# The last 224 rows of a weight in two transfers over 25 and 7 partitions instead of four over 8

## Chip, cores, metric

The kernel runs on one core of a Trainium2 chip. The metric is the device time of one execution in microseconds. Before the change it is 664.14 us, the median of 3 runs (664.11 to 664.20).

## The reference, cut to what matters

One decoding step: a cached attention block and a gated MLP read the same normalised `x`, and their outputs are added to `x`. Four sequences, one token each, 32 heads, 4096 cached positions of 128 values, all in bf16.

```python
def _A_ref(x, k_cache, v_cache, wq, wo):          # k_cache, v_cache: (4, 32, 4096, 128)
    ...                                           # q = x @ wq; softmax(q k^T) v; @ wo
def _B_ref(x, w_in, w_sp, b_sp, w_out):           # w_in: (640, 1728), w_out: (864, 640)
    z = _gelu(jnp.einsum('bsd,df->bsf', x, w_in))
    ...
    return jnp.einsum('bsf,fd->bsd', z1 * g, w_out)
xn = _layernorm(x, axis=-1)
return x + _A_ref(xn, ...) + _B_ref(xn, ...)
```

The two caches are 268 of the 282 MB that are read. The change touches the last 224 of the 864 rows of `w_out`, 0.29 MB.

## The kernel before

All large loads go out on one queue, in program order, into five slots of SBUF. The first 640 rows of `w_out` go to 128 partitions, five rows to each. The other 224 are 32 times 7 rows; they go to the lowest 32 partitions of a buffer that is later used for something else. They come in four transfers: transfer `r` covers partitions `r`, `r+4`, ..., `r+28`.

```python
FA = 5
FR = (Fh - FA * P) // 32                     # 7
# ...
nc.sync.dma_start(out=wq, in_=A_wq.rearrange("(p c) n -> p c n", c=DC))
# ...
nc.sync.dma_start(out=w_in, in_=B_w_in.rearrange("(p c) f -> p c f", c=DC))
nf = FA * P
# ...
nc.sync.dma_start(out=w_out, in_=B_w_out[0:nf, :].rearrange("(p c) n -> p c n", p=P))
w_rest_t = ktpool.tile([P, NKT], F32, tag="kT", name="w_rest")
w_rest = w_rest_t[:32].bitcast(BF16)[:, 0:FR * NOUT].rearrange("p (c n) -> p c n", c=FR)
# ...
w_rest_d = B_w_out[nf:Fh, :].rearrange("(i r c) n -> r i c n", r=4, c=FR)
for r in range(4):
    nc.sync.dma_start(out=w_rest[r:32:4], in_=w_rest_d[r])
# ...
load_unit(seq[0])                            # the first unit of k_cache, 8.39 MB
# ... much later: the only readers of w_rest
for fc in range(FC):
    # ...
    for hf in range(NH):
        nc.tensor.matmul(proj[...], lhsT=uT[:n, fc, 0:nb],
                         rhs=(w_out[:, fc] if fc < FA else w_rest[:, fc - FA])[:, hf * NO2:(hf + 1) * NO2], ...)
```

The rest of the kernel is a loop over 16 units of k and 16 of v, and at the end the projection with `wo`.

Of the kernel before, what the change touches and what calls it, by code (L numbers as in the profile page):

```python
# [16 lines left out]
def kernel(  # L17
# [19 lines left out]
    nc = tc.nc  # L37
# [18 lines left out]
    Fh = F2 // 2  # L56
    FA = 5
    FR = (Fh - FA * P) // 32
# [56 lines left out]
    nf = FA * P  # L115
# [3 lines left out]
    w_rest = w_rest_t[:32].bitcast(BF16)[:, 0:FR * NOUT].rearrange("p (c n) -> p c n", c=FR)  # L119

    NB = 32 * FC
    z_at = n_in + FA * NOUT
    w_rest_d = B_w_out[nf:Fh, :].rearrange("(i r c) n -> r i c n", r=4, c=FR)
    for r in range(4):
        nc.sync.dma_start(out=w_rest[r:32:4], in_=w_rest_d[r])


    seq = [("k", u) for u in range(B)]
# [212 lines left out]
    for fc in range(FC):  # L341
        n = P if fc < FA else 32
        nb = B if fc > 1 else 32
        r0 = 64 * (fc % 2)
# [202 lines left out]
    for c in range(HG):  # L547

        p = part.get(c, 0)
# [41 lines left out]
```

## Time and profile before

| | before |
|---|---|
| time | 664.14 us |
| span of the profiled run | 662.5 us |
| read from memory | 282.25 MB, 426 GB/s over the span |
| busiest compute engine | DVE, 54% |
| last piece of `wo` landed | 658.98 us |

The prediction below shows the lines of the page that say what bounds the kernel.

Some numbers below come from the records of single DMA packets and of single semaphore counts (one for each engine that has finished its part of a transfer), which stand in the trace. Of such counts a large load has 16, each of the four small transfers 8, each of the two loads of `x_res` 4. The records don't name the engine; the strands, of which the prediction speaks, are my own stringing by time. "Loss" of a strand means: the time from the end of its last `w_out` packet to the end of its eighth packet of the first k load, less eight times 2.414 us. In the kernel before it is 1.37 us on the eight strands with small packets and 0.01 us on the other eight.

### The profile page before, as it was taken

What the parts mean: (1) busy time and instruction counts of PE and PEld (TensorE: products, weight loads), DVE (VectorE), ACT (ScalarE), POOL (GpSimd) and SP (SyncE); (2) the same over time, 40 slices, a digit from 0 to 9 for tenths busy, and PEclk for the clock granted to TensorE, in tenths of its full rate; (3) what the DMA queues carried; (4) which work ended last, traced back from release to release, by engine and by line L of the source; (5) the groups of instructions that cost most, each with busy time, mean ns of one, the idle gap of its engine ahead of it and who ended that gap; (6) DMA issues with size and microseconds to landing.
All of it is one profiled execution on the core that took longest, in us unless ns stands there. A gap on an engine that the chain in (4) does not pass through costs nothing.

```text
span 662.5 us, 5421 instructions
## 1 busy us (share of the span) xinstructions
PE 292.9 (44%) x2297; PEld 106.5 (16%) x2297; DVE 360.1 (54%) x275; ACT 78.4 (12%) x162; POOL 20.3 (3%) x64
## 2 busy tenths in 40 slices
PE   0636666256072556225336054533506254623245
PEld 0111122112021122111112022111202112211122
DVE  2249899556191759618256286745619185951112
ACT  0300000530100000530200000071010000053200
POOL 6210000000000000000000000000000000000000
PEclk9858768678577587677859596756958759667767
DMA  9999999999999999999999999999999999999996
GB/s 371 463 424 427 426 444 437 435 436 416 443 432 423 439 418 442 433 439 440 423 420 435 432 421 452 433 424 431 431 436 444 428 431 415 445 432 437 418 419 262
DMA packets 6901, 282.61 MB, mean 427 GB/s; under 512 B 808, under 2 KB 1084, under 8 KB 1468
## 3 DMA queue, kind: packets, MB, share of 16 engines
q1 hardware_dynamic: 6856, 282.25, 98.8%
q8 instruction: 18, 0.29, 0.2%
q14 instruction: 7, 0.06, 0.0%
q10 hardware_dynamic: 20, 0.01, 0.0%
HBM read 282.25 MB, written 0.01 MB: 426 GB/s over the span
## 4 chain that ended last, share of the span: by engine, by line
DMA 74%; DVE 11%; issue 11%; PE 2%; ACT 1%; SPq 0%; DVEq 0%; ACTq 0%
DMA kv<-in_A_k_cache_dram 64%; DVE kT L367 11%; DMA kv<-in_A_v_cache_dram 5%; DMA kv<-in_A_wo_dram 3%; DMA kv<-in_A_wq_dram 2%; PE O L449 2%; ACT xd L432 0%; ACT Zb L413 0%; ACT p L421 0%; DVE pT L425 0%; PE last_a L553 0%; DVE m L385 0%; PE S L378 0%; SPq L169 0%; PE misc L390 0%
## 5 line engine op out<-in xcount | busy, mean ns | idle before, releaser
L367 DVE STREAM_TRANSPOSE kT<-kv 128x2048 f32<-128x2048 f32 x128 | 282.8, 2276 | 124.7 <-DMA kv<-in_A_k_cache_dram 124.7
L378 PE MATMUL S<-kT,QZ 128*32 128x512 bf16 x1024 | 187.9, 500 | 230.6 <-DVE kT L367 230.6
L378 PEld LDWEIGHTS <-QZ 128*32 128x32 bf16 x1024 | 60.3, 111 | 353.4 <-issue 332.6
L449 PE MATMUL O<-kv,Zb 128*32 128x512 bf16 x1024 | 73.6, 451 | 58.2 <-DMA kv<-in_A_v_cache_dram 38.0
L458 DVE TENSOR_TENSOR om<-O,Mk 128x512 f32<-128x512 f32 x15 | 10.4, 692 | 109.0 <-PE O L449 109.0
L413 ACT ACTIVATE Zb<-xd,MkE 32x256 bf16<-32x256 bf16 x116 | 52.9, 498 | 110.4 <-PE O L449 109.0
L421 ACT ACTIVATE p<-S,negmax 128x512 bf16<-128x512 f32 x8 | 5.4, 683 | 400.6 <-DVE negmax L399 400.6
L449 PEld LDWEIGHTS <-Zb 128*32 128x32 bf16 x1024 | 32.9, 112 | 97.4 <-issue 55.8
L472 PE MATMUL misc<-R,SelR 128*32 128x128 f32 x32 | 6.4, 281 | 30.0 <-DVE R L459 28.4
L353 POOL COPY QZ<-qT 32x32 bf16<-32x32 bf16 x16 | 5.1, 318 | 390.6 <-PE S L378 389.9
L432 DVE COPY xd<-pT 32x256 bf16<-32x256 bf16 x44 | 16.0, 365 | 0.8
L459 DVE TENSOR_REDUCE R<-om 128x128 f32<-128x512 f32 x15 | 15.3, 1019 | 0.5
L432 ACT COPY xd<-pT 32x256 bf16<-32x256 bf16 x20 | 12.3, 614 | 5.6 <-DVE pT L425 5.2
L425 DVE STREAM_TRANSPOSE pT<-p 128x1024 bf16<-128x1024 bf16 x4 | 5.0, 1245 | 6.3 <-ACT p L421 6.3
L472 PEld LDWEIGHTS misc<-R,SelR 128*32 128x32 f32 x32 | 2.2, 107 | 37.8 <-DVE R L459 26.0
L385 DVE TENSOR_REDUCE m<-S 128x2 f32<-128x1024 f32 x4 | 4.9, 1225 | 5.5 <-PE S L378 5.5
L274 PE MATMUL q<-kv,xnT 128*32 128x512 bf16 x40 | 4.5, 630 | 6.9 <-DMA kv<-in_A_wq_dram 6.9
L461 DVE TENSOR_SCALAR R<-O,Mk 128x128 f32<-128x128 f32 x1 | 0.4, 351 | 12.5 <-PE O L449 12.5
L282 DVE CAST kv<-q 128x512 bf16<-128x512 f32 x1 | 0.7, 692 | 11.1 <-PE q L274 11.1
L390 PE MATMUL misc<-dg,ones_f 128*128 128x256 f32 x8 | 3.2, 488 | 7.6 <-DVE dg L387 7.6
L475 DVE SCALAR_TENSOR_TENSOR om<-misc,rinv,SelH 32x1024 bf16<-32x1024 f32 x4 | 5.1, 1271 | 2.0 <-PE misc L472 2.0
L437 PE MATMUL misc<-rowsum,SelPe 128*32 128x1 f32 x16 | 2.1, 202 | 9.0 <-ACT p L421 9.0
(102 smaller groups left out, 78.2 us busy)
## 6 DMA issues: line engine op xcount, KB each, us to landing
kv<-in_A_k_cache_dram SPq DMA_DIRECT2D x8, 4096.0 KB
kv<-in_A_v_cache_dram SPq DMA_DIRECT2D x1, 6144.0 KB
kv<-in_A_wq_dram SPq DMA_DIRECT2D x1, 5120.0 KB
kv<-in_A_wo_dram SPq DMA_DIRECT2D x3, 1280.0 KB
kv<-in_B_w_in_dram SPq DMA_DIRECT2D x1, 2160.0 KB, 19.9
kv<-in_A_v_cache_dram SPq DMA_DIRECT2D x1, 2048.0 KB
kv<-in_B_w_out_dram SPq DMA_DIRECT2D x1, 800.0 KB
kv<-in_A_wo_dram SPq DMA_DIRECT2D x1, 640.0 KB, 22.0
```

The lines of the kernel that those rows point to most:

```text
L353: nc.gpsimd.tensor_copy(out=QZ[r0:r0 + 32, :, :, :, 8 + 8 * hp], in_=qT[32 * g:32 * g + 32, NE * hp:NE * hp + NE].rearrange("p e a b -> p ...
L367: nc.vector.transpose(kT[:].rearrange("p (t r) -> p t r", r=32), kw)
L378: nc.tensor.matmul(S_ps[32 * q:32 * q + 32, e], lhsT=QZ[:, b, 2 * kh + w, e, w0:w0 + 32], rhs=kb[:, i, :, e, :, w], start=(b == 0 and k < ...
L413: nc.scalar.activation(out=dst, in_=src, func=ACT.Copy, scale=mk)
L421: nc.scalar.activation(out=p_bf[:, :, e, :], in_=S_ps[:, e], func=ACT.Exp, bias=negmax[:, e:e + 1], scale=scale, accum_out=rowsum[:, e:e + 1])
L425: nc.vector.transpose(pT[:].rearrange("p t h x -> p (t h x)"), p_bf[:].rearrange("p t e m -> p (t e m)"))
L432: op(out=xd[32 * hp:32 * hp + 32, :, q, :], in_=pT[32 * q:32 * q + 32, :, hp, :].rearrange("p t x -> p x t"))
L449: nc.tensor.matmul(O_ps[32 * q:32 * q + 32, :, :], lhsT=Zb[b % 2][:, w].rearrange("p h c -> p (h c)"), rhs=vv[:, w * 4 * Dh:(w + 1) * 4 * ...
L458: nc.vector.tensor_tensor(out=om4[:], in0=O_ps[:], in1=Mk4[:, :, None].to_broadcast((P, 4, Dh)), op=ALU.mult)
L459: nc.vector.tensor_reduce(out=R, in_=om4[:].rearrange("p c d -> p d c"), axis=AX.X, op=ALU.add)
L472: nc.tensor.matmul(oh[:], lhsT=SelR[:, b].rearrange("p h b -> p (h b)"), rhs=state["R"][:, b, :], start=(b == 0), stop=(b == B - 1))
L475: nc.vector.scalar_tensor_tensor(out=om[:], in0=oh[:, None, :].to_broadcast((G, HG, Dh)), scalar=state.pop(("rinv", g))[:, 0:1], in1=MkH[: ...
```

## The change

The intent: two transfers instead of four, over runs of partitions, with fewer issues. The four transfers over 8 partitions counted 8 landings each.

```diff
-    w_rest_d = B_w_out[nf:Fh, :].rearrange("(i r c) n -> r i c n", r=4, c=FR)
-    for r in range(4):
-        nc.sync.dma_start(out=w_rest[r:32:4], in_=w_rest_d[r])
+    w_rest_d = B_w_out[nf:Fh, :].rearrange("(p c) n -> p c n", c=FR)
+
+    for r0, r1 in ((0, 25), (25, 32)):
+        nc.sync.dma_start(out=w_rest[r0:r1], in_=w_rest_d[r0:r1])
```

The same rows land in the same partitions.

## The prediction

> **What bounds the kernel now.** I read the page from the top: slices, queues, chain; then the queue's own timeline, then the single packets and landings.
>
> From the page of the kernel before (the line of DMA is busy tenths per slice; the queue line is packets, MB, share of the time of 16 engines):
>
> ```profile
> DMA  9999999999999999999999999999999999999996
> q1 hardware_dynamic: 6856, 282.25, 98.8%
> DMA 74%; DVE 11%; issue 11%; PE 2%; ACT 1%; SPq 0%; DVEq 0%; ACTq 0%
> kv<-in_A_v_cache_dram SPq DMA_DIRECT2D x15, 29.5
> w_rest<-in_B_w_out_dram SPq DMA_DIRECT2D x4, 70.0 KB
> ```
>
> The 16 DMA engines work without a break on one queue, and DVE, the busiest engine, has 54%. A bulk load lands 29.5 us after its issue although its own 8.39 MB need 19.4 us (128 packets of 65,536 B, 8 on each engine, 2.418 us each): 10 us of earlier work are always ahead of it. So neither the issues nor DVE bound this kernel, but the bytes that one DMA engine has to move. A packet of 65,536 B takes 2.418 us all through the trace, which is 27.1 GB/s per engine[...].
>
> The chain of waits, its last stretch (start, length, what):
>
> ```profile
> 635.85 22.32 DMA kv<-in_A_wo_dram
> 658.17 0.04 issue
> 658.21 0.43 PE last_a L553 x2
> 658.64 0.01 PE misc L553 x2
> 658.65 0.82 PE last_a L553 x4
> 659.47 0.02 issue
> 659.49 0.48 DVE o_bf L560
> ```
>
> The end is the landing of the last piece of wo, two matmuls, an addition, and the store. Each transfer counts as landed when its slowest engine is through, and[...] the end belongs to **the engine that is furthest behind**, not to the mean.
>
> The start, from the timeline of the queue that issues (start, length with its waits):
>
> ```profile
> 0.73 0.39 SPq L110 DMA_DIRECT2D kv<-in_A_wq_dram  x1
> 1.18 0.42 SPq L113 DMA_DIRECT2D kv<-in_B_w_in_dram  x1
> 1.64 0.57 SPq L117 DMA_DIRECT2D kv<-in_B_w_out_dram  x1
> 2.25 14.30 SPq L125 DMA_DIRECT2D w_rest<-in_B_w_out_dram  x4
> 16.60 36.15 SPq L161 DMA_DIRECT2D kv<-in_A_k_cache_dram  x3
> ```
>
> The four small transfers of the change hold the issuing queue from 2.25 to 16.55 us. In the waits of that queue 11.5 us of this are a wait for wq: the semaphores of the transfers come round after eight, and the fourth small one needs the semaphore of wq.
>
> [...]each of the four transfers over 8 partitions counted 8 landings, x_res over 4 partitions 4, all others 16. [...]
>
> **The change part by part.** The 32 partitions hold 7 rows of 640 bf16, 8,960 B each; such a packet takes 338 ns, and the packet that counts the semaphore 9 ns.
> - Before, engines 0 to 7 each move 4 of them: 4 x (338 + 9) = 1.39 us that engines 8 to 15 don't have.
> - After, engines 0 to 4 move 5 + 1 = 6: 6 x 338 + 2 x 9 = 2.05 us, so **+0.66 us**. Engines 5 and 6 move 1: 0.35 us, so -1.04. Engine 7 moves none: -1.39. Bytes, packets of data and everything later are the same.
> - Two issues of some 0.63 us fall away, and the wait of 11.5 us with them, since the semaphore of wq is next needed by the second load of k_cache. The first k load can be issued near 3.6 instead of 16.6 us. It gains nothing: the engines reach that load at 21 to 23 us, the landing times of the small transfers show.
> - The consumer of w_rest is a group of 14 matmuls at 36.7 us, after a chain on ACT, DVE and POOL; w_rest lands by 23.8 us. Some 12 us of slack.
>
> So only the tail of the most loaded engine counts. The packets don't name their engine, but each starts 3 to 6 ns before the end of the one ahead, so they can be strung into 16 strands by time (my own working from the packet records). Eight strands carry w_rest, four of them x_res as well, so these are engines 0 to 3. All strands have the same bulk; they differ by a start spread over 1.1 us, by w_rest, and by instruction fetches of 16,384 B (about 1.0 us each) and 8,192 B (0.3 us) that fall on some. The last packets end at 658.57 us on the latest strand, then 658.26 (one of engines 0 to 3), 658.26 (one of 8 to 15), 658.22 and 658.11 (both of 4 to 7). The fastest end near 654. The latest owes its place to a third 16 KB fetch at 633.7 us; the fetches go round eight strands in a fixed order, and by it this is one of engines 8 to 15, though at 628 us two strands meet and could be exchanged.
>
> Engine cost alone: 658.26 + 0.66 = 658.92 against 658.57 now, **+0.35 us**; if the latest strand is one of 0 to 4, +0.66.
>
> **Rivals.**
> [...]
> - *A faster start.* The queue is free 13 us earlier. That would help only if an engine had run dry; no strand has a gap other than fetches. No change in time.
> - *A balance that helps.* If the latest strand were engine 5, 6 or 7, its end would fall back by 1.0 to 1.4, but 658.26 + 0.66 on the other strand remains. So hardly below 664.1; a gain needs fetches that fall otherwise.
> - *Knock-on through buffers.* A later first k load delays DVE, and with it the issue of the third load at 52.4 us. The fastest engine would need it near 60 us; 2 us are lost in that slack.
>
> **Range and chances.** I weigh engine cost alone (664.14 + 0.35 to 0.66, so 664.5 to 664.8) with a third[...], the rest for luck with fetches[...]. Middle: 665.2 us, range 664.0 to 667.0. A change of 2% is 13.3 us, more than six times the largest term: within 2% with 0.985, slower 0.01, faster 0.005.
>
> **What would show it.** The two transfers should count 5 and 7 landings, with 32 packets of 8,960 B. The wait of the issuing queue for wq at this line should be gone, the first k load issued near 3.6 us, and landed no earlier than 43 us. [...] The spread between first and last engine of a landing should grow by 0.3 to 2.5 us right after w_rest and stay; bulk packets should keep 2.418 us. The last piece of wo should land (658.98 us before) later by the change in time. I am wrong if the end moves though that spread doesn't, if a strand runs dry, or if k isn't 5 and 7.

One rival, +0.7 to +2.2 us (664.8 to 666.4 us): that the partitions which are written count too. It was the estimate from an assumption, and it had a little over half of the weight. The sum: engine cost alone with a third, that rival with a little over half, the rest for luck with fetches and for a worse case of the rival, in the middle 665.2 us, range 664.0 to 667.0. The "largest term" there is the rival's 2.2 us. `k` is the number of engines that a transfer runs on, to be read from its landings.

The numbers of engines are names, here and in the expectations: "engines 0 to 7" are the eight strands that carry small packets in the kernel before, "0 to 3" the four of them that carry `x_res` too, "8 to 15" the eight strands without small packets.

That the semaphores come round after eight can be seen in the trace of the kernel before: its first eight transfers, `x`, `wq`, the two single values, `w_in`, `w_out` and two of the small ones, have a semaphore each. The third small one has that of `x`, the fourth that of `wq`, on which `wq` counted from 14.86 to 15.92 us and the small one from 23.28 to 23.72.

## More of the kernel before

One more view is needed for what follows: the stretch from 21 to 26 us, in which the four small transfers and the start of the first k load pass. The columns are the stretch, its length, the busy time of PE, PEld, DVE, ACT and POOL (with instructions), the granted clock, the share of the DMA engines, and GB/s. The share goes over 1; packets seem to count where they start. So only equal stretches should be compared.

```profile
core 0: us, PE busy (x) PEld busy (x) DVE busy (x) ACT busy (x) POOL busy (x), PEclk, DMA share, GB/s
21.00:26.00 5.00, 4.93 (x25) 1.07 (x24) 1.40 (x2) 0.69 (x2) 1.57 (x5) 1.00 1.26 540
```

What to see: 540 is the figure of an undisturbed stretch, with which the others are compared.

## The result

The changed kernel takes 665.51 us, the median of 6 runs (665.14 to 665.75), against 664.12 us (664.06 to 664.31) of the kernel before. The ratio is 1.002 with a 95% interval of 1.0007 to 1.0033, so it is the same within 2%, and slower by 1.4 us. A ratio is the mean time of one kernel's fast runs over that of the other's of the same rounds, so it isn't quite the ratio of the medians.

From the page of the kernel after (tenths of DMA, the queue line, the chain):

```profile
DMA  9999999999999999999999999999999999999996
q1 hardware_dynamic: 6836, 282.25, 98.9%
DMA 74%; DVE 11%; issue 11%; PE 2%; ACT 1%; SPq 0%; DVEq 0%; ACTq 0%
```

The same bytes, 20 packets fewer (the semaphore counts: 5 + 7 instead of 4 times 8). The page alone can't tell the two kernels apart.

The timeline of the issuing queue, after:

```profile
2.27 0.84 SPq L126 DMA_DIRECT2D w_rest<-in_B_w_out_dram  x2
3.15 51.53 SPq L162 DMA_DIRECT2D kv<-in_A_k_cache_dram  x3
```

The wait for `wq` is gone, and the first k load is issued at 3.15 us instead of 16.60. It lands 1.9 us later all the same. This is in the chain of waits, after:

```profile
3.15 42.16 DMA kv<-in_A_k_cache_dram
45.31 0.03 issue
...
636.02 22.80 DMA kv<-in_A_wo_dram
658.82 0.04 issue
...
660.89 0.03 issue
660.92 0.48 DVE o_bf L561
```

Add start and length in the first line: 45.31 us, where before had 16.60 + 26.78 = 43.38. The last addition starts at 660.92 instead of 659.49, 1.43 us later. So the whole loss is there at 45 us, and nothing is added to it in the 600 us that follow. The stretch of the small transfers, after:

```profile
21.00:26.00 5.00, 4.97 (x25) 1.04 (x24) 1.25 (x1) 0.72 (x2) 1.56 (x5) 1.00 1.22 408
```

408 instead of 540. The packet records say where it goes:

| 20 to 30 us | before | after |
|---|---|---|
| packets of 8,960 B, median and longest | 338, 338 ns | 385, 982 ns |
| packets of 65,536 B over 2,450 ns | 0 | 22, longest 4,202 ns |
| strands with most small packets: loss | 1.37 us (4 packets, 8 strands) | 3.26 to 3.77 us (6 packets, 5 strands) |
| strands with one small packet: loss | - | 2.11 and 2.17 us |
| the others: loss | 0.01 us | 1.61 us on one, 1.23 to 1.24 us on eight |

The last row is the surprise. Eight engines have nothing to do with the small transfers and each lost 1.23 us nevertheless. By number these should be the eight that had none before, 8 to 15 (and the strand with 1.61 us the one that had four and now has none); the records name no engine. (On one of the eight an instruction fetch falls into the interval; 1.55 us are taken off for it, 1.10 of the fetch and the rest on the large packet beside it.) The last packet over 2,450 ns starts at 25.5 us.

The landings of the last piece of `wo`: before, the last count came at 658.98 us and the next at 658.70; after, at 660.41 and 660.21. The two small loads of `x_res` near 608 us counted four landings each (before from 607.58 to 610.90 us) and so mark four engines, 0 to 3 by name, in the list of landings. By it, followed from landing to landing, the last count before isn't one of engines 0 to 3, and after it is.

### The profile page after: what moved, and what is told of

It is laid out like the page before. It is cut to its first block, busy times and chain, and to the rows that moved or that the text cites. A ratio compares the mean times of both kernels' runs of the same rounds, so it can differ in the third digit from the quotient of the medians.

```text
span 663.7 us, 5419 instructions
## 1 busy us (share of the span) xinstructions
PE 294.3 (44%) x2297; PEld 106.8 (16%) x2297; DVE 360.0 (54%) x275; ACT 78.4 (12%) x162; POOL 20.2 (3%) x64
## 4 chain that ended last, share of the span: by engine, by line
DMA 74%; DVE 11%; issue 11%; PE 2%; ACT 1%; SPq 0%; DVEq 0%; ACTq 0%
DMA kv<-in_A_k_cache_dram 66%; DVE kT L368 11%; DMA kv<-in_A_v_cache_dram 5%; DMA kv<-in_A_wo_dram 3%; PE O L450 1%; ACT xd L433 0%; ACT Zb L414 0%; PE last_a L554 0%; ACT p L422 0%; DVE pT L426 0%; DVE m L386 0%; PE S L379 0%; SPq L126 0%; PE misc L391 0%; SPq L117 0%
```

## The experiments

Theories when they were made:
- **Engine load**: only the small packets per engine matter. It should give +0.35 to +0.66 us.
- **Fair sharing**: engines that write neighbouring partitions at the same time hold each other up; nobody else loses anything.
- **Common stall**: such writes slow all 16 engines, also those that have no part in them.
- **Reads**: the changed kernel reads neighbouring blocks of 8,960 B at the same time, the one before every fourth, and memory serves that worse.
- **Early issue**: the first k load comes 13 us earlier into the queue and does the damage.

"Port theory" in the expectations is a name for the second and the third: that it matters which partitions are written. No record shows a port.

All 12 kernels had a median within 2% of before. Times are medians of fast runs, each with the kernel before in the same rounds.

### One transfer over 32 partitions

```diff
-    for r in range(4):
-        nc.sync.dma_start(out=w_rest[r:32:4], in_=w_rest_d[r])
+    nc.sync.dma_start(out=w_rest, in_=w_rest_d)       # w_rest_d as "(p c) n -> p c n"
```

> One transfer over 32 partitions, two packets on each of 16 engines[...]. Engine-count theory: the most loaded engines have 2 packets less, 0.7 us less on engines 0 to 7 and 0.7 more on 8 to 15: 664.1 to 664.8. [...] Common stall: more than 2 us on all.

Measured: 665.91 us against 664.16. The most even distribution over engines is 1.75 us slower, so engine load alone, which allowed 664.8 at most, is refuted. Twelve of sixteen strands lost 1.70 to 1.89 us, three more (one of these with a fetch) and one 1.42, though two packets need 0.69.

### Four transfers over 8 neighbouring partitions

```diff
-        nc.sync.dma_start(out=w_rest[r:32:4], in_=w_rest_d[r])
+        nc.sync.dma_start(out=w_rest[8 * r:8 * r + 8], in_=w_rest_d[8 * r:8 * r + 8])
```

> Four transfers over 8 partitions as before, 4 packets on each of engines 0 to 7, but over partitions 8r to 8r+7[...]. Engine-count theory (only packets per engine matter): nothing changes, 664.1. [...] Common-stall theory[...]: engines 8 to 15 lose over 1 us as well.

Measured: 666.17 us against 664.16, +2.01. Each of the eight strands has four small packets as before, but the partitions of a transfer lie side by side. The strands with small packets lost 3.15 to 3.6 us instead of 1.37. Of the strands without, which by fair sharing would lose nothing, five lost 1.80 to 1.81 us, one the same beside a fetch, and two less (1.41 and 0.72), which came to their last `w_out` packets later than the rest. The timeline of the queue and the stretch from 21 to 26 us of this kernel:

```profile
2.37 14.04 SPq L125 DMA_DIRECT2D w_rest<-in_B_w_out_dram  x4
16.45 38.23 SPq L161 DMA_DIRECT2D kv<-in_A_k_cache_dram  x3
```

```profile
21.00:26.00 5.00, 4.72 (x25) 1.04 (x24) 1.60 (x2) 0.59 (x1) 1.58 (x5) 1.00 1.23 368
```

368 GB/s, the lowest of all, with the first k load issued as late as before (16.45 us). So an early issue isn't needed for the stall.

### Reads and partitions crossed

This kernel changes the order of reads, rows and partitions crossed apart, and gives a wrong result: the partitions of before with the reads of the kernel above.

```diff
-    w_rest_d = B_w_out[nf:Fh, :].rearrange("(i r c) n -> r i c n", r=4, c=FR)
+    w_rest_d = B_w_out[nf:Fh, :].rearrange("(p c) n -> p c n", c=FR)
     for r in range(4):
-        nc.sync.dma_start(out=w_rest[r:32:4], in_=w_rest_d[r])
+        nc.sync.dma_start(out=w_rest[r:32:4], in_=w_rest_d[8 * r:8 * r + 8])
```

> Gives a wrong result on purpose. The partitions[...] of before, but transfer r reads the rows 8r to 8r+7 of 8960 B, one behind the other in memory as in the changed kernel, where before reads every fourth. Reading theory (the pattern of reads slows all engines): engines 8 to 15 lose over 1 us, first k load lands after 44.5 us, time 665.5 or more. Port theory: rows at 338 ns, bulk packets at 2418 ns, no loss on engines 8 to 15, first k load at 43.4 us, time 664.1 within 0.3.

Measured: 664.17 us against 664.22; relative error 0.576. No bulk packet took over 2,418 ns, every small one 338. The stretch:

```profile
21.00:26.00 5.00, 4.95 (x25) 1.07 (x24) 1.36 (x2) 0.71 (x2) 1.57 (x5) 1.00 1.26 541
```

The other half of the cross (also wrong, relative error 0.565) has the neighbouring partitions and the reads of before:

```diff
-        nc.sync.dma_start(out=w_rest[r:32:4], in_=w_rest_d[r])
+        nc.sync.dma_start(out=w_rest[8 * r:8 * r + 8], in_=w_rest_d[r])
```

> Gives a wrong result on purpose. The other half of the cross: the partitions of contig8[...], but each transfer reads every fourth row as before does. Reading theory: as before, 664.1, no loss on engines 8 to 15. Port theory: as contig8, engines 0 to 7 lose 3.1 to 3.6 us and engines 8 to 15 about 1.8, time 666.0 within 0.5.

Measured: 665.89 us against 664.22, +1.67. Of the strands without small packets six lost 1.44 to 1.45 us, one more beside a fetch, and one 0.66; the others lost about 2.8 to 3.1, less than the 3.1 to 3.6 that was expected.

```profile
21.00:26.00 5.00, 4.53 (x24) 1.07 (x24) 1.80 (x2) 0.59 (x1) 1.57 (x5) 1.00 1.24 404
```

The pair settles it: the loss goes with the partitions that are written, not with the addresses that are read. The reads may add a little (1.45 against 1.80 us), which these single profiles don't settle.

### One more small transfer, every fourth partition, first try

The kernel before and one transfer more, whose data nobody reads. I put it into a free stretch of the large buffer.

```diff
+    dum = at_slot(0, 5120, n_q + 8 * D + 2 * HG * Dh)
+    nc.sync.dma_start(out=dum[0:16:4], in_=B_w_out.rearrange("(p c) n -> p (c n)", c=8)[0:4])
```

> The kernel before and one more transfer behind the four (its data is not used): 10240 B to each of partitions 0, 4, 8, 12[...]. Engine-count theory and fair sharing: +0.39 us on engines 0 to 3, nothing on others; bulk packets at 2418 ns; time 664.1 to 664.5. Common stall by any small transfer: engines 8 to 15 lose time too.

Measured: 666.09 us against 664.16. This does not tell what it was made for. The timeline of the queue of this kernel:

```profile
2.14 14.37 SPq L125 DMA_DIRECT2D w_rest<-in_B_w_out_dram  x4
21.07 0.59 SPq L127 DMA_DIRECT2D kv<-in_B_w_out_dram  x1
21.70 32.81 SPq L163 DMA_DIRECT2D kv<-in_A_k_cache_dram  x3
```

The added transfer was given a wait for `w_in`, which lies in another slot of the same buffer (4.5 us in the waits of the queue; why it had to wait for that isn't shown), and was issued only at 21.07 us. With that the first k load came at 21.70 us, when the engines had run dry (385 GB/s from 21 to 26 us): the strands without small packets lost 1.0 to 2.3 us, and all 16 began the k load nearly together. It is a by-product worth having. It shows what running dry looks like, and that the slack of the first k load ends between 17.3 us (an issue that was harmless in the next run) and 21.7 us. It is also a warning: 15 of its large packets between 20 and 30 us took over 2,450 ns, the longest 3,262, with no small transfer to neighbouring partitions. So a slow packet alone is no sign of these. In the changed kernel the first k load was issued at 3.15 us and no strand ran dry, so its loss isn't this one.

### One more small transfer, every fourth partition, mended

The same idea with the target in partitions 32 and up of the buffer of `w_rest`, which are free at that time.

```diff
+    w_more = w_rest_t[32:52:4].bitcast(BF16)[:, 0:FR * NOUT].rearrange("p (c n) -> p c n", c=FR)
+    nc.sync.dma_start(out=w_more, in_=w_rest_d[0][0:5])
```

> The kernel before and one more transfer of five packets of 8960 B behind the four (its data is not used), to partitions 32, 36, 40, 44, 48[...]. Engine-count theory and port theory both: +0.35 us on engines 0 to 4 (five packets, 1.71 us in all), nothing on the others, the first k load is issued before 18 us; time 664.1 to 664.5. If any small transfer stalls all engines, engines 8 to 15 lose time.

Measured: 664.30 us against 664.22. Five strands carry five small packets and lost 1.71 us, three carry four and lost 1.37, eight lost 0.01; no packet was slow. The stretch:

```profile
21.00:26.00 5.00, 4.99 (x25) 1.05 (x24) 1.25 (x1) 0.62 (x2) 1.56 (x5) 1.00 1.25 535
```

One packet more on five strands, to every fourth partition, cost these its packet time (0.34 us) and nobody else anything, and hardly shows in the time (+0.08 us).

### The same over eight neighbouring partitions

```diff
+    w_more = w_rest_t[32:40].bitcast(BF16)[:, 0:FR * NOUT].rearrange("p (c n) -> p c n", c=FR)
+    nc.sync.dma_start(out=w_more, in_=w_rest_d[0][0:8])
```

> The kernel before and one more transfer of eight packets of 8960 B behind the four (its data is not used), to partitions 32 to 39[...]. Engine-count theory: +0.35 us on engines 0 to 7, nothing on the others, 664.3 within 0.3. [...] Common stall[...]: a quarter of contig8, so engines 8 to 15 lose about 0.4 to 0.6 us; 664.8 to 665.3.

Measured: 665.22 us against 664.22, +1.00. Strands without small packets lost 0.63 to 0.65 us (one has a fetch), those with them about 1.0 to 1.2 us more than before. The stretch:

```profile
21.00:26.00 5.00, 4.69 (x25) 1.05 (x24) 1.63 (x2) 0.59 (x1) 1.58 (x5) 1.00 1.18 450
```

Eight packets of 8,960 B, 72 KB in all, cost the kernel 1 us when they go to eight neighbouring partitions at once.

### The same over every fourth partition, from 36 on

```diff
+    w_more = w_rest_t[36:64:4].bitcast(BF16)[:, 0:FR * NOUT].rearrange("p (c n) -> p c n", c=FR)
+    nc.sync.dma_start(out=w_more, in_=w_rest_d[0][0:7])
```

> The kernel before and one more transfer of seven packets of 8960 B behind the four (its data is not used), to partitions 36, 40 to 60[...]. [...] Crowding theory[...]: [...]engines 8 to 15 lose little, under 0.2 us, and engines 0 to 6 about 0.35 to 0.7 us more than before; time 664.2 to 664.8.

Measured: 664.50 us against 664.13. (The crowding theory is that only writes to neighbouring partitions cost the other engines anything.) The eight strands without small packets lost 0.01 us; the longest bulk packet took 2,544 ns. Most of the others lost 1.71 to 1.74 us, as the strands with five small packets did in the run with partitions 32 to 48 (1.71). The stretch:

```profile
21.00:26.00 5.00, 5.00 (x25) 0.96 (x24) 1.25 (x1) 0.84 (x2) 1.57 (x5) 1.00 1.26 539
```

The difference in time, 0.37 us, isn't clear of noise (interval of the ratio 0.9991 to 1.0021). Seven packets to every fourth partition cost the other engines nothing, also one step further on (0.01 us); eight to neighbouring partitions, in the run above, cost each of them 0.64 us. A theory would have let them lose seven eighths of that, 0.56 us.

### Early issue, two tries that failed

Both try to issue the first k load early behind the four transfers of before. The first moved the two loads of single values ahead of that of `x`:

```diff
-    nc.scalar.dma_start(out=x_bf, in_=x_flat)
     sb_bf = const.tile([1, 2], BF16)
     nc.scalar.dma_start(out=sb_bf[:, 0:1], in_=B_w_sp)
     nc.scalar.dma_start(out=sb_bf[:, 1:2], in_=B_b_sp[None, :])
+    nc.scalar.dma_start(out=x_bf, in_=x_flat)
```

> The four matched transfers of before, and the two tiny scalar loads moved ahead of x, so that no transfer ahead of the first k load waits for wq. Early-issue theory (the earlier first k load is what slowed all engines): the first k load, issued near 4 us, lands late as in the changed kernel (45.3 instead of 43.4 us) and the time is near 665.5. Port theory: landing at 43.4 us, bulk packets right after w_rest at 2418 ns, time 664.1 within 0.3.

Measured: 664.24 us against 664.16, but the first k load was still issued at 16.78 us. The second try moved them behind the activation of `z`:

```diff
-    nc.scalar.dma_start(out=sb_bf[:, 0:1], in_=B_w_sp)
-    nc.scalar.dma_start(out=sb_bf[:, 1:2], in_=B_b_sp[None, :])
 ...
+    nc.scalar.dma_start(out=sb_bf[:, 0:1], in_=B_w_sp)
+    nc.scalar.dma_start(out=sb_bf[:, 1:2], in_=B_b_sp[None, :])
     one_bf = const.tile([1, P], BF16)
```

> Mends the first try at the early issue, in which the wait for wq stayed: the two tiny scalar loads now come after the activation of z, so the first k load waits only for x and is issued near 5 us behind the four matched transfers. Early-issue theory: engines 8 to 15 lose over 1 us right after w_rest and the time is near 665.5. Port theory: nothing lost, first k load at 43.4 us, time 664.1 within 0.3.

Measured: 664.18 us against 664.13, the first k load at 16.61 us. In both kernels the fourth small transfer again got the semaphore of `wq`, and in the second its issue waited for `wq` until 15.94 us. The order in which they are given out isn't that of the program: in the kernel before, `wq` has the second, though in the program both single values stand between `x` and it. So neither brought the early issue that it was made for, and they are no evidence on it. An early issue isn't needed for the stall: the two runs with four transfers over 8 neighbouring partitions and the one with a fifth of that kind show it with the first k load issued at 16.45 to 17.35 us. Whether an early issue alone costs or gains anything, also within the changed kernel, remains untried.

### Another size

Six chunks of `w_out` over 128 partitions leave 96 rows, in small packets of 3,840 B. First with the four transfers of before, as an attempt at a faster kernel:

```diff
-    FA = 5
+    FA = 6
```

> Six chunks of w_out over 128 partitions instead of five, so the rest is 96 rows in packets of 3840 B[...]. Worked out from the packet times: engines 0 to 7 have 0.39 us less than before, engines 8 to 15 0.38 more. If the latest engine is one of 8 to 15, as the order of the fetches says, the end moves by +0.4: 664.5; if it is one of 0 to 7, by -0.3: 663.8. No stall.

Measured: 664.54 us against 664.13, no faster. A small packet takes 149 ns; the loss of the strands with four is 0.61 us instead of 1.37, while every strand has 0.38 us more of `w_out`. The last piece landed at 659.35 us, 0.37 after 658.98. This fits the reading that the latest engine of the kernel before is one of 8 to 15, the eight without small packets, which get the 0.38 and no relief.

Then the same size with the two transfers of the change:

> The same six chunks with the two transfers of the change (25 and 7 partitions)[...]. If the stall goes with the bytes[...], engines 8 to 15 lose 3/7 of 1.23 us, so 0.53 us, and the time is 0.4 to 0.7 us over that of the six chunks[...]; if it goes with the number of packets, 1.2 us.

Measured: 664.94 us against 664.13 (interval of the ratio 1.0000 to 1.0025), and 0.40 over the six chunks with four transfers. Seven strands without small packets lost 0.33 to 0.34 us, where bytes in proportion would give 0.53 and packets in proportion 1.23. Neither reading fits; between these two sizes the stall shrinks faster than the bytes.

### All runs side by side

The loss is that of strands without small packets of this transfer; in the kernel with 32 partitions every strand has two, so there 0.69 is taken off.

| kernel | partitions of the small transfers | loss, us | last landing, us | time - before, us |
|---|---|---|---|---|
| before | every fourth | 0.01 | 658.98 | - |
| early issue, two tries that failed | every fourth | 0.01 | 658.87, 658.87 | +0.08, +0.05 |
| reads crossed, partitions of before | every fourth | 0.01 | 658.89 | -0.05 |
| five more, from 32 on | every fourth | 0.01 | 658.91 | +0.08 |
| seven more, from 36 on | every fourth | 0.01 | 659.18 | +0.37 |
| six chunks, four transfers | every fourth | 0.01 | 659.35 | +0.41 |
| six chunks, 25 + 7 | neighbours | 0.34 | 659.83 | +0.81 |
| eight more, 32 to 39 | every fourth; of the added one, neighbours | 0.64 | 659.92 | +1.00 |
| the change, 25 + 7 | neighbours | 1.23 | 660.41 | +1.39 |
| one more, first try (ran dry) | every fourth | 1.0 to 2.3 | 660.73 | +1.93 |
| 8 neighbours, reads of before | neighbours | 1.45 | 660.63 | +1.67 |
| 32 partitions at once | neighbours | 1.0 | 660.67 | +1.75 |
| 8 neighbours | neighbours | 1.80 | 660.89 | +2.01 |

In all of them the time is the last landing plus 5.0 to 5.4 us. Where a small transfer wrote neighbouring partitions, the last landing moved by at least what the strands without small packets lost near 22 us (1.91 us for 1.80, 0.94 for 0.64): what is lost there is still lost at 658 us.

Not tested: which of the two transfers of the change, the one over 25 partitions or the one over 7, costs the other engines their 1.23 us.

No version here beats the kernel before.

## Why the prediction was right

- *The bound.* Right. The strands show no pause at the start of the k load, before or after, and the loss of one to two us there is still in the time. But "a packet of 65,536 B takes 2.418 us all through the trace" was a premise too many: already in the kernel before, 31 of 3,456 took over 2.45 us, and in the changed one 44, of which 22 between 20 and 30 us, where before had none.
- *Five and seven engines.* Right: the two transfers counted 5 and 7 landings, with 32 packets of 8,960 B. ("All others 16", as it says of the kernel before, holds for the large loads only: `x` over 4 partitions counted 4.)
- *The wait for `wq`.* Right: it left that line, the first k load was issued at 3.15 us (3.6 expected), and it gained nothing.
- *Engine load, +0.66 us on engines 0 to 4.* Right by itself (0.34 us for one packet more, in the run with five more to every fourth partition), but the smaller part: those strands lost 1.9 to 2.4 us more than before.
- *The rival.* It is what happened: the strands with six small packets lose most, 3.26, 3.26, 3.27, 3.48 and 3.77 us, where the packets alone would take 2.05. The prediction gave this rival a little over half, and the latest of engines 0 to 3 lands 1.71 us later (660.41 against 658.70), within the +0.7 to +2.2 us. Why it should happen was an assumption and isn't shown.
- *The other strands.* Here the rival was wrong. Its estimate let engines 8 to 15 lose nothing, and each of them lost 1.23 us. That is why the spread of a landing, which should grow by 0.3 to 2.5 us and stay, grew from 2.10 to 2.76 us at the first k load but only from 4.48 to 4.57 at the end, while the end moved by 1.43: the fast engines were slowed too. By its own words ("I am wrong if the end moves though that spread doesn't") the prediction failed here, in the account of how the time is lost, though not in the time. *"Bulk packets should keep 2.418 us"* failed for the same reason; 22 of them took over 2,450 ns.
- *Small packets of 600 ns or more*, the rival's sign, were a poor one: only 4 of the 32 took that long. Most of the waiting sits in the bulk packets that follow.
- *Fetches.* Each of the 18 of 16,384 B took a DMA engine 1.00 to 1.11 us. That the engine with a third one ended last in the kernel before is the prediction's reading of the strands; it isn't sure, as strands can be exchanged where they meet.
- *The time.* 665.2 foretold, 665.51 measured, within 664.0 to 667.0. Part of that is luck: by the common stall alone the latest engine of before would land at 658.98 + 1.23 = 660.21 us, where a landing is indeed found, and one of 0 to 3 lands at 660.41 with the larger loss of the strands with six small packets, so that the two effects, one foreseen and one not, end within 0.2 us of each other.

How writes to neighbouring partitions hold up engines that have no part in them is not shown; no run watched their path.

## What to carry to other kernels

When a load goes to fewer than 128 partitions, try how they are dealt: here four transfers to every fourth partition, on eight engines (664.16 us), were better than one to 32 partitions at once, on sixteen (665.91 us). When a kernel is bound by its DMA engines, as this one with 98.8% of their time on one queue, count what each engine moves and look at the engine that is last; and look at the packets of engines that have no part in the change, for here writes to neighbouring partitions slowed them too (by 1.23 us in the change). Where a small experiment adds a transfer, look first at when it and the next were issued: a wait that came along with it can cost more than what it was to measure (1.93 us here, with 0.39 expected).
